# Attention and expert kernel on one core: the last 64 keys scored with 66 stationary columns, the maxima turned in the scores' shape

## Chip, cores and metric

One core of a Trainium2 chip runs the whole program. The metric is device microseconds of one execution; the profile is of one execution. Engines: PE is TensorE (PEld its loading of stationary operands), DVE is VectorE, ACT is ScalarE, POOL is GpSimd, and SP issues DMAs. Each engine takes its instructions in the order of the program.

## The reference

```python
# attention: batch 8, 8 heads, 576 positions, head size 64, float32
scores = (q @ k.T) / sqrt(64)
scores = where(block_i >= block_j, scores, -1e9)     # blocks of 64 positions
attn = exp(scores - scores.max(-1)); attn /= attn.sum(-1) + 1e-9
x = (attn @ v) -> (4608, 512)
# soft mixture: 8 experts, 4 slots each, width 1024
logits = x @ phi
d = softmax over the 4608 tokens; c = softmax over the 32 slots
slot_in = d.T @ x
slot_out[e] = relu(slot_in[e] @ w1[e]) @ w2[e]
x = c @ slot_out
# product block
a = x @ moe2_w1; b = x @ moe2_w2                     # 512 -> 1024 each
out = ((a * b) @ w3) @ w_out                         # 1024 -> 1024 -> 512
```

## The kernel before

The 64 heads of attention are taken as 32 pairs. Queries and keys lie transposed, one head of a pair on partitions 0 to 63 and the other on 64 to 127, so two matmuls of 64 rows run at once, one for each head. Scores stand with keys on the partitions and queries along the row. FP32 products are made from rounded parts: a high part (cast, L483, on ACT) and a low part (difference, L490, on POOL), and each product is three matmuls.

For each pair, `op_M` (L495) multiplies the high parts with queries on the partitions, four groups in four bank pairs, and `op_R` (L504, DVE) takes the maxima of 64 keys each. `op_l2` makes of them the running maximum that a query needs, ten columns. These must become rows: `op_mT` (L516) transposes them into one PSUM bank, `op_mc` (ACT) copies, and `op_mx` (L524) issues three small DMAs that put them into rows 0 and 64 of X. Rows 1 to 5 of X, and the tiles `CT`, are constants of the causal mask.

`op_Q` (L533) makes the scores in four units. In each unit a key tile has three matmuls a head and a fourth, `CT` times X, which subtracts the maximum and adds the mask. Unit 0 holds key tile 1 (queries 128 on, 448 columns) and the last keys, 512 to 575, which only 64 queries see. These last are scored with 128 stationary columns, keys 448 to 575, of which the first 64 are masked. `op_E` (ACT) takes the exponential of a unit, `op_P` (POOL) sums, `op_V` multiplies with the values, `op_SU` makes the row sums, and `op_sb` (DVE) gathers them. Every four pairs are a batch of the tokens; its logits, transposes and slot inputs run under the next pairs.

PSUM has eight banks. A unit or a maxima group takes a pair of them, other products one. The order of everything is made by a planner (`Plan`, L88): each operation has an engine, a duration, its predecessors, banks, and a due time from the tables `OFF`, `EARLY`, `LATE`, `TAIL` and `POST`. It simulates the engines and emits the program in the order found; a matmul's mode (rows for 64-row matmuls, cols, quarters, full) adds a cost where it changes.

The product block's weights don't depend on tokens. `background` (L949) unpacks 64-bit floats into 32-bit ones under the pairs: a load, four DVE operations, and an ACT square, 26 times, for w_out, the first two pieces of w3T, w1 and w2. The other 14 pieces of w3T follow the pairs (`op_rl`, `op_nq`, `op_n`), together with 16 windows of expert weights of 2 MB (`op_wl`). From w3T and w_out, `op_W` makes W = w3 w_out in 192 matmuls that fill TensorE where the plan has time. After the last expert the slots' a and b are multiplied for all slot pairs: `slot_product` (L1188) makes two products and their sum on DVE, and halves the columns of equal slots; `run` (L1212) multiplies this with W to H and then makes the output from products of the combine weights and H.

Where pairs 0 and 1 wait, `run` of the attention (L921) puts matmuls of zeros that keep TensorE busy.

Of the kernel before, what the change touches and what calls it, by code (L numbers as in the profile page):

```python
# [17 lines left out]
S = 576  # L18
# [9 lines left out]
SP = 640  # L28
# [3 lines left out]
def warm(nc, keep, ps, n, w=128):  # L32

    for _ in range(n):
# [3 lines left out]
OFF = dict(ld=(-3671.042, -1992.2911, -303.0511, -1589.0792), ldv=(-930.8255, -774.9205, -2694.8577, 3004.9495),  # L38
           cast=(2024.9564, 3492.1229, 4706.3225, 4642.3979), sub=(829.8094, 2265.7417, 2641.5476, 2007.6771),
           M0=(-206.0862, -217.4342, -265.7846, -210.5146), M1=(-171.9627, -155.0874, -208.7453, -200.1106),  # L40
           M2=(-127.28, -214.9706, -278.1956, -151.8956), M3=(-169.0631, -252.9726, -229.3314, -145.805),
           l2=(-2693.6488, -1083.0339, 305.268, -503.7642), mT=(-95.3927, -48.5566, -124.2345, -87.7389),
           Q0=(84.7224, 29.4226, 39.4315, 30.1907), Q1=(89.7578, 54.2034, 79.5471, 35.3739),
           Q2=(98.4373, 58.5153, 51.2166, 82.5414), Q3=(89.8008, 88.7918, 49.8111, 57.1466),
           P0=(-913.8297, 548.2446, -1367.0333, -777.5844), P3=(-741.4936, 304.0305, -2114.9437, -1607.1186),
           V1=(203.1097, 209.8759, 219.5606, 192.1869), V0=(210.9204, 105.6152, 105.8713, 102.9399),
           SU=(199.7409, 191.2759, 151.163, 120.8971), r=960.7404, sx0=2515.4131, sx1=596.7543, sx2=-224.853, sx3=1870.0829,
           lg=396.7265, lgT=458.8917, cm=1933.1093, cT=701.6961, LTm=-87.1704, dn=451.3287, xn0=454.2761, xn1=453.8451,
           xn2=454.1203, xn3=462.6411, xn4=453.5743, S=599.0796, b=972.45)
EARLY = dict(M=(-1939.2203, -1039.3961, -688.4126, -538.7845), m=(-1036.791, -811.8334, -353.2116, -479.9624),  # L50
           Q=(-544.7669, -532.4325, 0.6058, 2.9171))
LATE = dict(M0=(-16.3677, 49.8754, 121.1889, 106.9067), M1=(34.8112, -16.0442, 130.5073, 45.366),
           M2=(-51.968, -1.3651, 69.8318, 86.3003), M3=(15.7624, 30.6289, -20.4844, 74.7255),
           mT=(51.0406, -15.9257, 149.4984, 95.4908), Q0=(24.9312, 0.9292, 84.621, 21.3772),
           Q1=(34.3074, 5.1476, 72.0112, 23.5192), Q2=(43.4204, 156.7641, 97.6101, 59.7645),
           Q3=(96.7668, 43.761, 104.3689, 4.6122), V0=(73.0635, 78.2534, 59.9265, 67.87),
           V1=(88.439, 24.2563, -33.0555, -8.2603), SU=(47.2236, 52.2312, 59.474, 69.5294),
           P0=(-210.3803, 47.2262, -17.1057, -266.9367), P3=(-25.429, 138.4384, 270.5177, 147.8325), r=-70.1372,
           sx0=-899.6328, sx1=-289.9241, sx2=-157.185, sx3=-1390.0855, lg=58.1323, lgT=222.5747, cm=-2205.5693, cT=18.7186,
           LTm=262.8129, dn=136.0191, xn0=149.6667, xn1=149.7181, xn2=163.6786, xn3=152.9745, xn4=149.6899, S=78.0479)  # L60
TAIL = dict(ts0=55.039, ts1=202.9811, lp0=-73.3871, lp1=57.9615, lp2=92.4441, lp3=101.5796, lt0=13.4395, lt1=90.8232,
           lt2=147.4599, lt3=205.3071, lr0=-343.9437, lr1=23.7771, lr2=98.6037, lr3=141.9388, xp0=129.3181, xp1=247.1579,
           xp2=302.5411, xp3=232.2751, xv0=-298.7287, xv1=321.9726, xv2=413.8655, xv3=-86.0816, chain=305.4669, comb=862.7258)
POST = dict(zm=586.802, W=21.766, We=-46.7975, Wh=312.1576, L=320.647, end=1110.3234, gh=490.5089, wl1=514.8806,
           wl2=114.7633, wl3=350.3128, wl4=-14.0545, wl5=228.0647, wl6=283.632, wl7=180.7612, wl8=598.3248, wl9=-30.7145,
           wl10=-32.1815, wl11=340.3284, wl12=670.2797, wl13=574.1696, wl14=167.9497, wl15=458.1722, rl2=564.6351,
           rl3=415.347, rl4=385.1454, rl5=342.5668, rl6=343.7061, rl7=173.1379, rl8=480.8373, rl9=642.1142, rl10=833.6257,
           rl11=60.6455, rl12=855.0533, rl13=394.0873, rl14=443.1501, rl15=-201.4425, nn2=424.0058, nn3=518.5431,
           nn4=101.2576, nn5=394.7296, nn6=544.1525, nn7=325.031, nn8=-17.0662, nn9=96.1954, nn10=400.0281, nn11=-274.2212,
           nn12=406.7534, nn13=52.5124, nn14=262.381, nn15=-17.5859, ph0=84.5591, ph1=-202.3024, ph2=396.9223, ph3=-565.2237,  # L70
           ph4=395.4213, ph5=351.3727, ph6=617.1742, ph7=572.4085, ph8=653.9999, ph9=374.4742, ph10=862.6272, ph11=286.4333,
           ph12=89.271, ph13=-293.3737, ph14=181.7482, ph15=153.9457, wh0=219.6349, wh1=-487.9067, wh2=444.6471,
           wh3=688.3682, wh4=498.6715, wh5=634.0177, wh6=59.5096, wh7=133.4419)
LOOK = dict(PE=0.0, DVE=1203.38805, ACT=958.21088, POOL=239.37081, SP=467.41166)
WAIT = dict(PE=0.0, DVE=8162.43521, ACT=4947.91525, POOL=3536.23117, SP=12465.53057)
PERIOD, HELD, SLIP, WIN0, WIN1 = 100.0, 30, 0.1, 20, 29
BG0, BGS = 3.0, 1.0
TURN = {"rows": dict(cols=.14, full=.165, quarters=.1), "cols": dict(rows=.205, full=.1, quarters=.06),
        "quarters": dict(rows=.22, full=.03, cols=.06), "full": dict(rows=.147, cols=.05, quarters=.03)}
# [3 lines left out]
MX = ((.262, 1.14), (.199, 1.007), (.14, .73), (.23, .73))  # L83
QK = ((1.25, .92), (1.026, .92), (.583, .6), (.475, .495))
VD = (0.65, 2.06)


class Plan:  # L88
# [3 lines left out]
    def __init__(self, nb):  # L92
# [4 lines left out]
        for n in range(N):  # L97
# [6 lines left out]
            if n == 0:  # L104
                op("kl", "SP", 2.9, lat=2.3, due="ld", late=-7e4)
                op("kc", "ACT", 2.1, at("cast", "kl"), due="cast", late=.1)
# [14 lines left out]
            e, f = ("DVE", .5) if n == N - 1 else ("POOL", 1.)  # L121
# [41 lines left out]
        for j in range(26):  # L163
# [12 lines left out]
    def last(self, N):  # L176
# [4 lines left out]
        for i in range(2):  # L181
            op("ts", i, "PE", .33, [("sb", N - 2 + i)], 1, due=f"ts{i}")
            op("tr", i, "DVE", .5, [("ts", i)] + [("tr", 0)] * i, free="ts", due=f"ts{i}", late=.1)
# [193 lines left out]
class Attn:  # L377
# [62 lines left out]
    def constants(self):  # L440
# [10 lines left out]
        for t in self.xTb:  # L451
            nc.gpsimd.memset(t[64:128, :, S:SP], 0.0)
# [1000 lines left out]
```

## Time and profile before

| | us |
|---|---|
| three runs | 569.20, 571.18, 571.79 |
| median | 571.18 |
| profiled execution | 569.49 |
| its span, first to last instruction | 567.6 |

| engine | busy us | share of the span | instructions |
|---|---|---|---|
| PE | 550.2 | 97% | 5444 |
| PEld | 414.3 | 73% | 5444 |
| DVE | 393.6 | 69% | 716 |
| ACT | 320.9 | 57% | 624 |
| POOL | 334.1 | 59% | 242 |

The busy time of an engine is a mean over stages with different limits, so it is read by stretches: pairs up to about 318 us, expert weights and W up to 427, slot products and H up to 453, the output behind. Matmuls are pipelined and their ends are modelled; the distance between two starts says what one costs. A matmul of FP32 operands that isn't a transpose stands as two instructions. In a timeline row the first number is the start, the second the time from the first start to the last end, and a bracket gives idle time before it and what ended that.

### The profile page before, as it was taken

To read this page: it belongs to the slowest core of one execution; us is meant where nothing else is said; L and a number is where in the kernel's file an instruction comes from. 1 tells how busy PE (TensorE), PEld (TensorE's weight loads), DVE (VectorE), ACT (ScalarE), POOL (GpSimd) and SP (SyncE) were. 2 spreads that over 40 slices of the span, in tenths; PEclk is the share of its full clock that TensorE was granted. 3 is DMA by queue.
4 is the path that set the end of the run, shared out by engine and by line. 5 is a ranking of instruction groups with operands and counts; after the bars stand their busy time and mean duration, and the time that the engine had idled before them with its cause. 6 is when DMAs were issued, how large, how long until landed. Compare 5 with 4: busy or idle time off the path is not lost.

```text
span 567.6 us, 13929 instructions
## 1 busy us (share of the span) xinstructions
PE 550.2 (97%) x5444; PEld 414.3 (73%) x5444; DVE 393.6 (69%) x716; ACT 320.9 (57%) x624; POOL 334.1 (59%) x242
## 2 busy tenths in 40 slices
PE   5999999999999999999999998998999999999997
PEld 3887878787878787878777763563667668888885
DVE  6678877888888988978870888105749776646550
ACT  4656758577686686785866653223532355544451
POOL 5887997987979979979977543103441013323230
PEclk9899999999999999999999998998999999999999
DMA  8355866566558466466354989999722037558622
GB/s 253 92 169 161 238 255 197 160 200 191 176 170 233 138 209 188 160 199 199 117 163 166 384 308 380 429 426 421 286 64 76 1 116 261 192 189 263 200 101 112
DMA packets 39289, 116.96 MB, mean 206 GB/s; under 512 B 5420, under 2 KB 15644, under 8 KB 37160
## 3 DMA queue, kind: packets, MB, share of 16 engines
q1 hardware_dynamic: 39224, 116.07, 59.4%
q8 instruction: 43, 0.70, 0.5%
q14 instruction: 22, 0.18, 0.1%
HBM read 105.75 MB, written 10.45 MB: 205 GB/s over the span
## 4 chain that ended last, share of the span: by engine, by line
PE 85%; DMA 6%; DVE 4%; ACT 2%; POOL 1%; issue 1%; DVEq 0%; POOLq 0%; ACTq 0%; SPq 0%
PE ps L542 20%; PE ps L1287 16%; PE ps L575 15%; PE ps L1066 6%; PE ps L502 5%; PE ps L591 4%; DMA s<-in_w3T 4%; PE ps L1224 3%; PE ps L697 3%; PE ps L1108 2%; DMA raw<-in_qk 2%; PE ps L640 2%; PE ps L1289 1%; PE ps L746 1%; PE ps L1087 1%; PE ps L518 1%
## 5 line engine op out<-in xcount | busy, mean ns | idle before, releaser
L506 DVE TENSOR_REDUCE tc<-ps 128x10 f32<-128x640 f32 (+2 forms) x128 | 122.5, 987 | 33.4 <-PE ps L502 25.8
L550 ACT ACTIVATE s<-ps 128x1024 f32<-128x1024 f32 (+2 forms) x128 | 102.9, 838 | 44.7 <-PE ps L542 34.5
L542 PE MATMUL ps<-set 64*128 64x320 f32 (+4 forms) x1152 | 112.8, 305 | 0.0
L542 PEld LDWEIGHTS ps<-set 64*128 64x128 f32 x1152 | 90.6, 187 | 5.0 <-issue 1.7
L490 POOL TENSOR_TENSOR set<-raw,set 128x1152 fp32r<-128x1152 f32 x32 | 84.9, 2657 | 7.8 <-ACT set L483 5.8
L560 POOL TENSOR_TENSOR tc<-tc,s 128x384 f32<-128x384 f32 (+1 forms) x63 | 80.7, 1281 | 7.0 <-ACT s L550 3.6
L560 POOL TENSOR_TENSOR tc<-s,s 128x640 f32<-128x640 f32 x32 | 49.9, 1560 | 30.4 <-ACT s L550 24.0
L575 PE MATMUL ps<-s,xw 128*64 128x320 f32 (+3 forms) x528 | 63.7, 383 | 0.0
L542 PE MATMUL ps<-shift 64*128 64x320 f32 (+4 forms) x384 | 58.5, 301 | 0.0
L1287 PE MATMUL ps<-H,pB 128*128 128x512 f32 x216 | 53.7, 395 | 0.4 <-POOL pB L1267 0.4
L1267 POOL TENSOR_TENSOR pB<-wx,pB 128x384 fp32r<-128x384 f32 x12 | 16.1, 1342 | 64.4 <-ACT pB L1262 64.4
L1287 PE MATMUL ps<-H,pA 128*128 128x512 f32 x216 | 53.2, 395 | 0.2 <-DVE H L1331 0.2
L502 PE MATMUL ps<-set 64*128 64x320 f32 (+4 forms) x384 | 48.3, 325 | 3.2 <-ACT set L483 3.0
L575 PEld LDWEIGHTS ps<-s,xw 128*64 128x64 f32 x528 | 34.6, 137 | 22.6 <-issue 0.7
L1294 ACT COPY s<-ps 128x512 f32<-128x512 f32 x36 | 21.1, 586 | 51.0 <-PE ps L1289 50.9
L1287 PEld LDWEIGHTS ps<-H,pB 128*128 128x128 f32 x216 | 40.6, 189 | 10.7 <-POOL pB L1267 1.1
L1287 PEld LDWEIGHTS ps<-H,pA 128*128 128x128 f32 x216 | 40.6, 188 | 10.3 <-DVE H L1331 0.5
L483 ACT CAST set<-raw 128x1152 fp32r<-128x1152 f32 x31 | 35.7, 1153 | 4.0 <-DMA raw<-in_qk 4.0
L502 PEld LDWEIGHTS ps<-set 64*128 64x128 f32 x384 | 31.5, 193 | 8.4 <-ACT set L483 3.5
L542 PEld LDWEIGHTS ps<-shift 64*128 64x128 f32 x384 | 36.8, 187 | 0.5
L1040 DVE TENSOR_SCALAR ps<-s 128x512 int32<-128x512 int32 x14 | 9.7, 692 | 34.1 <-DMA s<-in_w3T 33.9
L981 POOL TENSOR_TENSOR s<-vt,s 128x512 fp32r<-128x512 f32 x14 | 17.9, 1281 | 23.6 <-ACT s L983 23.6
(264 smaller groups left out, 1036.7 us busy)
## 6 DMA issues: line engine op xcount, KB each, us to landing
win<-in_moe_w SPq DMA_DIRECT2D x13, 2048.0 KB
raw<-in_qk SPq DMA_DIRECT2D x32, 576.0 KB
vt<-in_moe_w SPq DMA_DIRECT2D x16, 512.0 KB
out<-s SPq DMA_DIRECT2D x16, 512.0 KB
shift<-rr SPq DMA_DIRECT2D x56, 144.0 KB
s<-in_w3T SPq DMA_DIRECT2D x14, 512.0 KB
xw<-in_v SPq DMA_DIRECT2D x22, 320.0 KB
xw<-in_moe_w SPq DMA_DIRECT2D x3, 2048.0 KB
```

The costliest lines, as they stand in the source:

```text
L483: self.nc.scalar.copy(hi, self.raw[n])
L490: self.nc.gpsimd.tensor_tensor(lo, self.raw.pop(n), hi.bitcast(F32), op=ALU.subtract)
L502: self.nc.tensor.matmul(ps[:, h, o:o + kn], lhsT=qh[r, q0:q0 + 128], rhs=kh[r, k0:k0 + kn], start=True, stop=True)
L506: self.nc.vector.tensor_reduce(self.bmb[n % 2][:, :, o:o + m // 64], self.st.pop(("M", n, i))[:, :, 0:m].rearrange("p h (n k) -> p h n k", ...
L542: self.nc.tensor.matmul(ps[:, h, o0:o0 + w], lhsT=lt[r, k] if i < 3 else lt[r], rhs=rt[r, q0:q0 + w], start=i == 0, stop=i == 3)
L550: self.nc.scalar.activation(out=out, in_=ps[:, :, 0:sum(g[3] for g in self.UNITS[u])], func=AF.Exp, scale=SCALE)
L560: eng.tensor_tensor(acc[:, :, lo:hi], a, b, op=ALU.add)
L575: mm(ps[64 * h:64 * h + 64, q0 - lo:q1 - lo], lhsT=v[:, 128 * j + 64 * h:128 * j + 64 * h + 64], rhs=pt[:, h, o:o + q1 - q0], start=j == 0 ...
L591: mm = lambda g, o, rhs, **k: self.nc.tensor.matmul(ps[32 * g:32 * g + 32, o:o + rhs.shape[-1]], lhsT=one, rhs=rhs, **k)
L1066: self.nc.tensor.matmul(self.st["W", f], lhsT=a[:, o], rhs=b, start=j == 0, stop=j == 23)
L1287: nc.tensor.matmul(ps, lhsT=a[:, k, r], rhs=b[:, k], start=k + i == 0, stop=False)
L1294: nc.scalar.copy(o[:, h], bank(u, t))
```

## The change

Unit 0 of the scores starts with one mask product of 512 columns for key tile 1 and the last keys together. X and the constants grow to 640 columns for that: the last 64 queries' columns stand twice. The last keys follow with 66 stationary columns (keys 510 to 575; the two extra rows are masked), then the 448 columns of tile 1. The value rows of the last keys move to partitions 2 to 65. From pair 8 on, the first maxima group also uses 66 columns.

The maxima are turned, for pairs 2 to 31, by two transposes of 64 rows and 66 columns into a pair of banks, and moved by four DMAs. For pairs 0 and 1, ten FP32 matmuls with one stationary column each put each maximum row onto one partition, and ACT (`mc`) and DVE (`mk`) copy from there to X without a DMA.

Two more pieces of w3T go into the background (28 in place of 26). The halving in `slot_product` goes; the first H chunk is scaled by a column `own` instead (`op_ow`). In `run` the copy of X moves behind slice 7's cast. All tables of due times and some planner costs have new values.

```diff
             for i, (d, e) in enumerate(QK):
                 wait = at("Q0") if i else old(n - 2, "V1", "V0", "SU", "P0", "P1", "P3")
-                op(f"Q{i}", "PE", d, at("sub", "mx") + wait, 2, mode="rows")
+                op(f"Q{i}", "PE", d, at("sub") + moved + wait, 2, mode="rows")
...
-            op("mT", "PE", .109, at("l2") + (old(n - 2, "mx") or [("kl", 0)]), 1)
-            op("mc", "ACT", .148, at("mT"), free="mT", due="mT")
-            op("mx", "SP", .625 * 3, at("mc") + old(n - 2, *quarter("Q")) + ([("kc", 0)] if n == 0 else []), lat=2., due="mT", load=.3)
+            if n < 2:
+                op("mT", "PE", 1.3, at("l2") + [("kl", 0)], 2, mode="quarters")
+                op("mc", "ACT", 1.2, at("mT") + [("kc", 0)], due="mT")
+                op("mk", "DVE", 1.2, at("mT") + [("kc", 0)], free="mT", due="mT")
+            else:
+                op("mT", "PE", .12, at("l2") + (old(n - 2, "mx") if n > 3 else []), 2, mode="rows")
+                op("mc", "ACT", .17, at("mT"), free="mT", due="mT")
+                op("mx", "SP", .6 * 4, at("mc") + old(n - 2, *quarter("Q")), lat=2., due="mT", load=.3)
+            moved = at("mx") if n > 1 else at("mc", "mk")
...
-        for j in range(26):
+        for j in range(28):
...
-                op("zm", i, "POOL", .5, win[i])
+                op("zm", i, "POOL", .5, win[i] + [("pl", 3)] * (i == 0))
...
-            if i > 1:
+            if i > 3:
                 op("rl", i, "SP", .43, free[i] if i < 8 else [("W", 24 * (f - 4) + 12 * g + 11)], lat=2.5, load=1.25, due=f"rl{i}")
...
+            m = 66 if c == 0 and n > 7 else 128
             for h in range(2):
                 r = slice(64 * h, 64 * h + 64)
-                self.nc.tensor.matmul(ps[:, h, o:o + kn], lhsT=qh[r, q0:q0 + 128], rhs=kh[r, k0:k0 + kn], start=True, stop=True)
+                self.nc.tensor.matmul(ps[0:m, h, o:o + kn], lhsT=qh[r, q0:q0 + m], rhs=kh[r, k0:k0 + kn], start=True, stop=True)
...
-        self.nc.tensor.transpose(ps, self.m.pop(n).rearrange("p h w -> p (h w)"), self.ident)
+        if n < 2:
+            for w in (0, 1, 2, 3, 4):
+                for h in range(2):
+                    o = 128 * (w % 4)
+                    self.nc.tensor.matmul(ps[32 * h:32 * h + 1, w // 4, o:o + 128], lhsT=m[:, 5 * h + w:5 * h + w + 1], rhs=self.ident, start=True, stop=True)
+        else:
+            for h in range(2):
+                r = slice(64 * h, 64 * h + 64)
+                self.nc.tensor.transpose(ps[0:66, h, 0:64], m[r], self.ident[r, r])
+
+    def rows(self, eng, n, h):
+        ps, X = self.mt[n], self.Xb[n % 2][64 * h:64 * h + 1]
+        p = slice(32 * h, 32 * h + 1)
+        eng(X[:, 64:S], ps[p, 0, 0:512])
+        eng(X[:, S:SP], ps[p, 0, 448:512])
+        eng(X[:, 0:64], ps[p, 1, 0:64])
...
+        self.nc.sync.dma_start(out=X[0:65:64, S:SP], in_=t[3:9:5, 64:128])
         self.nc.sync.dma_start(out=X[0:65:64, 0:64], in_=t[4:10:5, 0:64])
...
+        if u == 0:
+            for h, r in two:
+                mm(h, 0, 512, self.CT[r, 1], X[r, 128:SP], start=True, stop=False)
+            for lt, rt in terms:
+                for h, r in two:
+                    mm(h, 448, 64, lt[r, 510:S], rt[r, 512:S], 66, start=False, stop=False)
+            for i, (lt, rt) in enumerate(terms):
+                for h, r in two:
+                    mm(h, 0, 448, lt[r, 128:256], rt[r, 128:S], start=False, stop=i == 2)
+            return
...
+    def op_ow(self, i, _):
+        self.own = self.attn.small[:, 60:61]
+        self.nc.vector.tensor_reduce(self.own, self.keep["ident"][:, 0:128:4], axis=AX.X, op=ALU.add)
+        self.nc.vector.tensor_scalar(self.own, self.own, -0.5, 1.0, op0=ALU.mult, op1=ALU.add)
...
             nc.vector.tensor_tensor(G, G, T, op=ALU.add)
-            own = cols(G)[:, 0, :, 0]
-            return nc.vector.tensor_scalar(own, own, 0.5, None, op0=ALU.mult).ins
...
                 for i in range(8):
                     h_last(i)
+            if f == 7:
                 nc.scalar.copy(X, Hp[4])
...
-            nc.scalar.copy(Hhi[:, k], Hp[k])
-            nc.vector.tensor_tensor(Hlo[:, k], Hp[k], Hhi[:, k].bitcast(F32), op=ALU.subtract)
+            if k == 0:
+                nc.scalar.mul(Hhi[:, 0], Hp[0], self.own)
+                nc.vector.scalar_tensor_tensor(Hlo[:, 0], Hp[0], self.own, Hhi[:, 0].bitcast(F32), op0=ALU.mult, op1=ALU.subtract)
+            else:
+                nc.scalar.copy(Hhi[:, k], Hp[k])
+                nc.vector.tensor_tensor(Hlo[:, k], Hp[k], Hhi[:, k].bitcast(F32), op=ALU.subtract)
```

## Rows read from the trace of the kernel before

**Rows 1.** Stretch; busy us of PE, PEld, DVE, ACT, POOL; clock; DMA share, GB/s

```profile
0.00:26.00 26.00, 19.90 (x164) 14.64 (x166) 17.19 (x37) 13.38 (x17) 17.10 (x20) 0.87 0.61 188
...
180.30:218.80 38.50, 38.50 (x528) 31.02 (x526) 33.58 (x62) 27.98 (x54) 33.26 (x23) 1.00 0.61 187
...
360.00:400.00 40.00, 37.70 (x254) 20.98 (x251) 9.98 (x15) 8.93 (x21) 5.09 (x4) 0.91 1.00 421
```

**Rows 2.** Waits, 26 to 296 us: us in total, times, longest

```profile
ACT s L550 <- PE ps L542: 32.2, 55, 1.6
```

**Rows 3.** TensorE's timeline, one unit 0: start, us, engine, line, operation

```profile
209.41 0.77 PE L542 MATMUL ps<-set 64*128 64x448 f32 x6
...
210.22 0.41 PE L542 MATMUL ps<-set 64*128 64x64 f32 x6
210.47 0.28 PE L542 MATMUL ps<-shift 64*128 64x64 f32 x2
210.58 0.54 PE L502 MATMUL ps<-set 64*128 64x320 f32 x6
```

**Rows 4.** TensorE's timeline, the end of one pair's value products

```profile
63.00 0.28 PE L579 MATMUL ps<-s,xw 128*64 128x64 f32 x4
63.11 0.82 PE L575 MATMUL ps<-s,vb 128*64 128x256 f32 x8
```

**Rows 5.** TensorE's timeline, one turn of maxima between other transposes

```profile
200.38 0.27 PE L518 MATMUL ps<-ident,wx 128*10 128x128 f32 x1
200.50 0.27 PE L697 MATMUL ps<-ident,wx 128*64 128x128 f32 x1
```

**Rows 6.** Timeline of the first 22 us

```profile
10.21 0.28 PE L518 MATMUL ps<-ident,wx 128*10 128x128 f32 x1
...
14.48 0.64 PE L502 MATMUL ps<-set 64*128 64x320 f32 x2 [2.98 <-ACT set L483]
...
17.04 1.32 PE L542 MATMUL ps<-set 64*128 64x448 f32 x6
```

**Rows 7.** Chain that ended last: start, us, engine and line, instructions

```profile
79.26 1.46 PE ps L640 x64
...
427.17 16.85 PE ps L1224 x72
...
467.38 2.79 PE ps L1287 x12
```

**Rows 8.** Timeline of all engines, 411 to 470 us: a copy of 512 columns

```profile
445.94 0.59 ACT L1321 COPY tc<-ps 128x512 f32<-128x512 f32 x1 [2.61 <-PE ps L1228]
```

**Rows 9.** DVE's timeline, 300 to 400 us

```profile
388.64 0.69 DVE L1040 TENSOR_SCALAR ps<-s 128x512 int32<-128x512 int32 x1 [32.16 <-DMA s<-in_w3T]
```

**Rows 10.** TensorE's timeline, 318 to 430 us

```profile
346.34 1.17 PE L1066 MATMUL ps<-raw,s 128*128 128x512 f32 x4 [2.15 <-DVE vt L1046]
```

**Rows 11.** Timeline of all engines again, slot products and what follows

```profile
423.37 1.58 POOL L981 TENSOR_TENSOR s<-wO,s 128x512 fp32r<-128x512 f32 x1 [7.10 <-ACT s L983]
...
423.84 1.17 DVE L1199 TENSOR_SCALAR g_stage<-g_stage 128x32 f32<-128x32 f32 x1
...
428.15 1.78 DVE L1195 TENSOR_TENSOR g_stage<-tc 128x512 f32<-128x512 f32 x1
...
433.81 0.68 DVE L1197 TENSOR_TENSOR g_stage<-g_stage 128x512 f32<-128x512 f32 x1
434.52 0.20 DVE L1199 TENSOR_SCALAR g_stage<-g_stage 128x32 f32<-128x32 f32 x1
434.62 0.68 DVE L1194 TENSOR_TENSOR g_stage<-tc 128x512 f32<-128x512 f32 x1
...
446.42 0.62 ACT L1206 CAST g_stage<-g_stage 128x512 fp32r<-128x512 f32 x1
...
447.10 1.22 PE L1224 MATMUL ps<-s,g_stage 128*128 128x512 f32 x3 [0.34 <-ACT g_stage L1206]
```

**Rows 12.** The page's costliest groups: exponentials of the scores

```profile
L550 ACT ACTIVATE s<-ps 128x1024 f32<-128x1024 f32 (+2 forms) x128 | 102.9, 838 | 44.7 <-PE ps L542 34.5
```

More of the change, by code (lines that the diff above doesn't have):

```diff
@@ L61 @@
[L61 to L73, printed above, removed]
@@ L76 @@
+LOOK = dict(PE=0.0, DVE=1443.82951, ACT=879.71342, POOL=478.25372, SP=447.13586)
+WAIT = dict(PE=0.0, DVE=10616.85007, ACT=6722.41331, POOL=7334.5673, SP=12439.66901)
 PERIOD, HELD, SLIP, WIN0, WIN1 = 100.0, 30, 0.1, 20, 29
 BG0, BGS = 3.0, 1.0
-TURN = {"rows": dict(cols=.14, full=.165, quarters=.1), "cols": dict(rows=.205, full=.1, quarters=.06),
-        "quarters": dict(rows=.22, full=.03, cols=.06), "full": dict(rows=.147, cols=.05, quarters=.03)}
+TURN = {"rows": dict(cols=.14, full=.165, quarters=.1), "cols": dict(rows=.14, full=.1, quarters=.06),
+        "quarters": dict(rows=.15, full=.12, cols=.06), "full": dict(rows=.147, cols=.05, quarters=.03)}
@@ L105, in __init__ @@
                 op("kl", "SP", 2.9, lat=2.3, due="ld", late=-7e4)
-                op("kc", "ACT", 2.1, at("cast", "kl"), due="cast", late=.1)
+                op("kc", "ACT", 1.9, at("cast", "kl"), due="cast", late=.1)
             op("sub", "POOL", 2.6, at("cast"))
@@ L120, in __init__ @@
             op("P1", "POOL", .96, at("P0"), due="P0", late=.1)
-            e, f = ("DVE", .5) if n == N - 1 else ("POOL", 1.)
+            e, f = ("DVE", .8) if n == N - 1 else ("POOL", 1.)
             op("P3", e, 1.51 * f, at("P0", "E2"))
@@ L182, in last @@
             op("ts", i, "PE", .33, [("sb", N - 2 + i)], 1, due=f"ts{i}")
-            op("tr", i, "DVE", .5, [("ts", i)] + [("tr", 0)] * i, free="ts", due=f"ts{i}", late=.1)
+            op("tr", i, "DVE", .35, [("ts", i)] + [("tr", 0)] * i, free="ts", due=f"ts{i}", late=.1)
         for p in range(NP_B):
@@ L189, in last @@
             op("lr", p, "DVE", .48, [("lt", p), ("tr", p // 3)] + [("la", p - 1)] * (p > 0), free="lt", due=f"lr{p}")
-            op("la", p, "DVE", .27 if p == 0 else .5, [("lr", p)] + [("la", p - 1)] * (p > 0), due=f"lr{p}", late=.1)
+            op("la", p, "DVE", .4 if p == 0 else .7, [("lr", p)] + [("la", p - 1)] * (p > 0), due=f"lr{p}", late=.1)
             op("xp", p, "PE", .545, [("lp", p)], 2, due=f"xp{p}")
@@ L203, in last @@
         op("wT", 0, "PE", .1, [("mS", 0), ("wM", 0)], due="chain", late=.45)
-        op("wb", 0, "DVE", 1.3, [("wT", 0), ("we", 0)], free="wM", due="chain", late=.55)
+        op("wb", 0, "DVE", 1.58, [("wT", 0), ("we", 0)], free="wM", due="chain", late=.55)
         op("ws", 0, "PE", .15, [("wb", 0)], 1, due="chain", late=.7)
-        op("wr", 0, "DVE", .3, [("ws", 0)], free="ws", due="chain", late=.75)
+        op("wr", 0, "DVE", .44, [("ws", 0)], free="ws", due="chain", late=.75)
         op("mI", 0, "PE", 1.13, [("mC", 0)] + [("xv", p) for p in range(NP_B)], 1, mode="quarters", due="chain", late=.6)
@@ L282, in experts @@
         op("aT", 0, "PE", .4, [("ac", 0)], 1, due="end", late=.3)
-        op("aa", 0, "ACT", 1., [("aT", 0)], due="end", late=.4)
-        op("ad", 0, "DVE", 1., [("aT", 0)], due="end", late=.5)
+        op("aa", 0, "ACT", .85, [("aT", 0)], due="end", late=.4)
+        op("ad", 0, "DVE", .85, [("aT", 0)], due="end", late=.5)
         op("af", 0, "SP", 0.01, [("aa", 0), ("ad", 0)], lat=0., free="aT", due="end", late=.6)
         op("g0", 0, "POOL", .4, [("L2", 7)], due="end")
+        op("ow", 0, "DVE", .3, [("L2", 6)], due="end")
         for f in range(4):
```

162 lines of the change are left out of this document (94 added, 68 removed).

## Prediction

> **What bounds the kernel now.** I read the busy time by stage first [rows 1], then the waits [rows 2], then TensorE's timeline. While the 32 head pairs run, TensorE is busy for all of the 38.50 us of a batch of four pairs (one of the eight is shown), at the full clock (granted share 1.00); DVE has 33.58, POOL 33.26, ACT 27.98. ACT's largest wait in that stretch is for TensorE's scores (32.2 us in 55 waits) [rows 2], so the engines behind TensorE stand waiting for it. In this stage a microsecond of TensorE's program order is a microsecond of the span. Three others are bounded otherwise. Before 17 us TensorE waits for data, and the clock's mean is 0.87 [rows 1]. From 360 to 400 us the DMA share is 1.00 at 421 GB/s. From 446 to 467 us a chain through ACT, DVE and POOL is last (the end term below).
>
> **How a score unit is paid.** Two matmuls, one for each head, run at once on 64 rows each; I call that a step. [Rows 3] show unit 0 of one pair. The four steps of 448 columns go from 209.41 to 210.22: 0.81, or 0.20 each. The steps of 64 columns come next, and the last takes from 210.47 to 210.58: 0.11. Streaming 64 columns should take 64/448 of 0.20, 0.03; the 0.11 is the loading of the next step's 128 stationary columns, which such a short step can't hide. The four short steps show 0.36 because the first one's load lay under the mask's 448 columns; the fourth's successor pays its load in the next unit. So 0.81 + 4 × 0.11 = 1.25. With 64 stationary columns, [rows 4] have four matmuls, two steps, from 63.00 to 63.11: 0.055 each.
>
> **(a) Unit 0, all 32 pairs.** After: one mask step of 512 columns (512/448 of 0.20 = 0.23); two steps that wait for 66 columns (taken as those of 64, 0.055 each); one that waits for the 128 columns of the first 448 (0.11); three of 448 (0.61). Sum 1.06, so 0.19 less a pair: 32 × 0.19 = **6.1 us**. The 66-column load itself is in no row. If it costs like 128, the sum is 0.23 + 0.33 + 0.61 = 1.17, 0.08 less (2.6 us in all); if it hides wholly, 0.23 + 0.06 + 0.11 + 0.61 = 1.01, 0.24 less (7.7). I take the row of 64, since 66 is nearest to it. All of this lies on TensorE's order, the path. The 66 columns in the maxima products (pairs 8 on) I cost at nothing: that load already lies under a step of 256 columns and the next load stays at 128; without that cover it would be 0.055 × 24 = 1.3.
>
> *A rule that speaks against (a).* In the rows, halving the columns halves the step. The Trainium skill (TensorE: Matmul & The Clock Gate, Weight-path perf modes) says that fast weight load is on with 128 weights of a type other than FP32. If it were on here, 66 columns would lose it, and (a) would give no more than its lower bound, 2.6; the trace shows no sign of it, 0.11 against 0.055.
>
> **(b) Turning the maxima, pairs 2 to 31.** Now one transpose on the whole array; between others of that shape it costs 0.12 (200.38 to 200.50) [rows 5]. After, two transposes of 64 rows run at once, in the scores' shape; their 66 columns hide under the step before, and the next step's 128 are exposed: 0.06 to 0.11. That gives 0 to 0.05 for each of 30, and the turn may go between scores without changing the array's shape. I take **0.8 us**, between 1.5 gained and 1.5 lost (0.05 the other way, should it stand between steps of another shape). SP issues a fourth small transfer of the rows for each such pair; SP issues nothing else that is late here. The mask now wants the rows 0.6 us earlier in the unit, first and not last. In the due times of the diff the turn stands more than half a pair ahead of its scores.
>
> **(c) Pairs 0 and 1.** Today the turn of pair 0 stands at 10.21, its rows go by DMA, and the first scores begin at 17.04, behind pair 2's maxima products (14.48, which waited for the cast) [rows 6]. After, five steps of two FP32 matmuls of 128 columns: [rows 7] give 1.46 for 64 instructions, four at once, 768 columns in each of four column strips, so 640 columns take 1.2, or 2.4 at the lower clock. Then ACT and DVE copy three pieces each at once; one of 512 columns takes ACT 0.59 [rows 8], so 0.6 to 1.8 for three, 1.1 taken. Scores begin near 13.1 (12.0 to 14.4): 3.9 earlier. Pair 2's products, 2.6 at the low clock (1.3 at full), now stand behind instead of ahead, and the second turn is 1.2 of TensorE's order: 3.9 − 1.3 − 1.2 = **1.4 us**. Bounds: 3.2 gained where the second turn falls in idle time; 1.7 lost where turns run at the low clock and DVE's three copies, with pair 1's maxima queued behind them, hold pair 1's scores up.
>
> **(d) Two more pieces of w3T in the background (28, not 26).** Eight DVE operations of 0.69 [rows 9] and two ACT squares move under the scores: DVE has 4.9 us idle in each batch [rows 1], which hides them; without that cover 5.5. They leave the stretch from 310 to 346 us, where DVE also carries the last batch's chain and where TensorE stood 2.15 for such a piece (346.34) [rows 10]. Their 1.05 MB are 2.5 us at 421 GB/s, counted only if the queue is full at that time. What is late next is the last expert weights: DVE later waits 32.16 for a w3T piece behind them in the queue [rows 9], and those bytes stay. So I take **2.0 us**: bounds 4.7 (2.15 + 2.5) and 1.0 lost (the zeros in the first expert window wait for POOL's split of piece 3).
>
> **(e) The halving in the slot products.** Eight DVE operations go; one took 0.20, and from the sum before it to the next product was 0.71 + 0.10 (433.81, 434.52, 434.62) [rows 11]. A sum followed at once by the next product should take about 0.6, the interval without a dependence: 0.2 × 7 = 1.4 of DVE. TensorE hides that up to 444 us: 72 matmuls in 16.85, 0.234 each, against 0.232 in the product loop [rows 7]. It counts behind that, where ACT's cast for slice 7 (446.42) stands behind the copy of X (0.59 at 445.94), and TensorE waits 0.34 for it (447.10) [rows 8, 11]; the copy is now issued after the cast. The chain behind starts up to 1.4 + 0.59 + 0.34 = 2.3 earlier. I take **1.5 us**, bounds 2.3 and 0; the scale in the first H copy and difference changes no operation count.
>
> *A rule weighed.* The first halving took 1.17, ending with POOL's split (423.37 + 1.58) [rows 11]. The Trainium skill (SBUF — State Buffer, Who interferes with whom) says that DVE and POOL share a port pair and that the later one waits for the whole of the other's instruction, also for an operation with two SBUF inputs. The trace agrees: a product at 428.15 took 1.78. Then 0.97 doesn't go with the halving but passes to the product behind it; counting it as gained would make the sum 1.0 larger. I don't count it.
>
> **The sum.** 6.1 + 0.8 + 1.4 + 2.0 + 1.5 = 11.8. The profiled execution is 569.49 (span 567.6 and 1.9 around it), so 557.7; the median of the three runs is 571.18, 0.3% above it, so on that scale **559.4**. All bounds together would be 19.4 gained to 1.6 lost, less likely than any one.
>
> **Rivals.**
> - *66 columns load no faster than 128* (the rule above is one way): (a) is 2.6, time 562.9. Against it: [rows 4]. Chance 0.10.
> - *Another engine is the bound at once.* POOL is at 33.26 of 38.50, DVE at 33.58 and more with (d). For it: POOL's sums lie between exponentials and the row sums in one order. Against it: the waits [rows 2], and 4.9 us idle against 0.9 saved a batch. Then (a) and (b) give nothing: 566.3. Chance 0.12.
> - *Slower: the turn's pair of banks.* The turn takes two of eight PSUM banks in place of one. If all four pairs are held when it comes up, TensorE's order stands until an exponential empties one: 0.838 on average [rows 12]. At 0.6 for each of 30 turns that is 18 us, 577; it decides from 11.8/30 = 0.39 a turn. Against it: ACT waits for TensorE [rows 2], so pairs come free early. Chance 0.08.
> - *The new order gives the gain back.* All due times change, so every operation may move. 0.35 us of waiting a pair eats 11 us: 568.5 to 571. For it: TensorE shows no idle time to win by order alone, only to lose. Chance 0.10.
>
> **How the numbers follow.** My forecast has 0.60, with its own range of 553 to 565. A measurement of this kernel can tell about 0.5% from no change, 568.3 to 574.0. Faster: 0.60 + 0.10 + 0.12 = 0.82. Same 0.10. Slower 0.08. The range of 8 in 10 takes in the forecast's bounds and the rivals to 566.3 and leaves out the last two: 551 to 567.5.
>
> **What would show it.** (a) right: from the mask's start to the next unit 1.0 to 1.1, short steps 0.055, and a batch of about 37.6 in place of 38.5. Wrong: short steps of 0.11. (b): the line of the turn with two entries a pair among scores, and TensorE never idle before it; the banks' rival shows as TensorE waiting for ACT there. (c): first scores near 13. (d): no idle time for DVE's pieces near 340, the last expert window landing earlier after the end of the pairs. (e): no wait at slice 7, and the product loop starting earlier after slice 0. A batch still at 38.5 with TensorE idle would make the prediction wrong at its main term.

## The result and the profile after

The kernel after takes 564.64 us (median of four, 563.02 to 565.62) against 571.48 for the kernel before (569.20 to 571.95): a ratio of 0.9889, interval 0.9854 to 0.9923. That is 6.8 us by the medians and 4.4 to 8.3 by the interval, where 11.8 were forecast. The profiled execution took 564.84, its span is 562.9 (before 567.6). One of the 12 executions of run 3 below took 1328 us and is not in its ratio.

Marks on TensorE's timeline, each the start of the first instruction named, tell where the time went:

| mark | before | after | difference |
|---|---|---|---|
| first scores | 17.04 | 17.55 | +0.5 |
| row sums of pair 0 | 27.06 | 26.11 | −1.0 |
| row sums of pair 24 | 253.15 | 248.68 | −4.5 |
| last matmuls of scores | 311.50 | 305.18 | −6.3 |
| first expert | 337.39 | 340.83 | +3.4 |
| first product of H | 427.17 | 423.27 | −3.9 |
| steady product loop | 467.38 | 462.11 | −5.3 |
| end of the span | 567.6 | 562.9 | −4.7 |

The pairs gain, the stretch from the last scores to the first expert gives 9.8 back, and from there to H 7.3 return. The 0.6 lost in the loop is no part of the change: twelve of its matmuls take 3.04 here and 3.02 before, but also 3.04 in run 1, whose loop is that of before, and 3.02 in runs 6 and 12, whose loop is that of after.

Stretches of after, columns as in [rows 1]:

```profile
0.00:26.00 26.00, 22.10 (x204) 15.13 (x204) 19.24 (x44) 15.54 (x24) 18.25 (x23) 1.00 0.57 187
172.51:210.75 38.24, 38.10 (x530) 29.96 (x526) 33.53 (x62) 28.19 (x56) 32.99 (x22) 1.00 0.60 188
...
360.00:400.00 40.00, 34.89 (x244) 19.11 (x243) 11.19 (x18) 10.94 (x25) 8.82 (x7) 0.96 1.02 427
```

The batch shown is from one row sum to that of four pairs later. It is 38.24, and TensorE, busy for all 38.50 before, now stands for 0.14 of it. Over five batches the mean is 38.04, against 38.59 before: 0.55 less, where 0.9 were forecast. From 360 to 400 us TensorE is busy for 34.89 in place of 37.70: the loads of the experts still fill the queue (share 1.02), and TensorE has less to do while it waits for them. From the row sums of pair 4 to those of pair 24, by distances between starts, the scores take 1.99 less than before, the turns 2.36 less, and everything else 1.6 more, of which 0.5 is in the maxima products: 2.75 in 20 pairs, 0.14 a pair, where 0.22 were forecast.

TensorE's timeline of after, a turn and one unit 0 (they answer to [rows 3] and [rows 5]):

```profile
204.95 0.25 PE L538 MATMUL ps<-ident,wx 64*66 64x64 f32 x2
205.00 0.60 PE L571 MATMUL ps<-set 64*128 64x256 f32 x6
...
205.93 0.40 PE L571 MATMUL ps<-shift 64*128 64x512 f32 x2
206.17 0.99 PE L571 MATMUL ps<-set 64*66 64x64 f32 x12
206.99 0.37 PE L513 MATMUL ps<-set 64*128 64x448 f32 x2
```

From the mask's start to the next unit 1.06, the number forecast; the turn takes 0.05. (The group of twelve merges the six short matmuls with the six of 448 columns.)

The start of after, TensorE's and DVE's timelines:

```profile
11.23 2.30 PE L534 MATMUL ps<-ident,wx 128*1 128x128 f32 x20
15.08 0.67 PE L513 MATMUL ps<-set 64*128 64x320 f32 x6 [1.55 <-ACT set L493]
15.68 1.26 PE L534 MATMUL ps<-ident,wx 128*1 128x128 f32 x20
...
17.55 0.49 PE L571 MATMUL ps<-shift 64*128 64x512 f32 x2
```

```profile
10.79 0.25 DVE L525 TENSOR_REDUCE wx<-tc 128x10 f32<-128x90 f32 x1
10.95 2.94 DVE L517 TENSOR_REDUCE tc<-ps 128x16 f32<-128x1024 f32 x3
13.92 0.69 DVE L543 CAST shift<-ps 1x512 fp32r<-1x512 f32 x1
```

Both turns and pair 2's products (15.08) stand ahead of the first scores, and DVE's copies stand behind 2.94 us of pair 1's maxima. The clock of 1.00 that the view gives for the first 26 us needs care. The trace of after has no entry of the granted clock before 13.6 us (that of before none before 6.2), and the view counts such time as full. The steps say otherwise. Three matmuls of zeros, before and after:

```profile
7.42 0.49 PE L35 MATMUL ps<-zeros 128*128 128x256 bf16 x3 [0.66 <-DVE tc L506]
```

```profile
7.49 0.80 PE L35 MATMUL ps<-zeros 128*128 128x256 bf16 x3 [0.26 <-DVE tc L517]
```

The last two stand 0.213 apart in after, 0.109 in before. So after ran at the lower level from about 7.5 to 13.6 us, ahead of its first scores; in before the entries have that level from 13.0 to 19.8 us, across them.

The 192 products W of the output weights (`op_W`, L1115 after, L1066 before) by stage: from 300 us to the first expert, to the start of the last expert's last matmul, to the first product of H. Columns: stretch, its length, busy us and number on PE, the same on PEld, clock, DMA share, GB/s. First before, then after:

```profile
300.00:337.39 37.39, 7.03 (x24) 4.05 (x24) 1.00 0.80 310
337.39:410.43 73.04, 35.41 (x124) 23.12 (x124) 0.93 0.93 381
410.43:427.17 16.74, 11.20 (x44) 7.96 (x44) 1.00 0.21 65
```

```profile
300.00:340.83 40.83, 12.14 (x42) 7.20 (x42) 1.00 0.70 260
340.83:408.82 67.99, 32.38 (x117) 20.25 (x116) 0.97 0.93 388
408.82:423.27 14.45, 8.91 (x34) 6.08 (x34) 1.00 0.20 61
```

After does 18 more of them ahead of the first expert and 10 fewer at the end, where nothing covers them: the last stretch is 2.29 shorter, and so is their busy time in it (11.20 and 8.91). This view explains most of what follows.

### The profile page after: what moved, and what is told of

It is laid out like the page before. It is cut to its first block, busy times and chain, and to the rows that moved or that the text cites. A ratio compares the mean times of both kernels' runs of the same rounds, so it can differ in the third digit from the quotient of the medians.

```text
span 562.9 us, 14019 instructions
## 1 busy us (share of the span) xinstructions
PE 545.0 (97%) x5444; PEld 404.0 (72%) x5444; DVE 393.8 (70%) x716; ACT 321.7 (57%) x628; POOL 331.4 (59%) x244
## 5 line engine op out<-in xcount | busy, mean ns | idle before, releaser
L571 PE MATMUL ps<-set 64*128 64x320 f32 (+4 forms) x1152 | 103.9, 298 | 1.4 <-ACT s L594 1.4
L571 PEld LDWEIGHTS ps<-set 64*128 64x128 f32 (+1 forms) x1152 | 82.6, 177 | 7.2 <-ACT s L594 1.9
L571 PE MATMUL ps<-shift 64*128 64x320 f32 (+3 forms) x320 | 51.6, 319 | 0.1
L1319 POOL TENSOR_TENSOR pB<-wx,pB 128x384 fp32r<-128x384 f32 x12 | 14.4, 1204 | 62.7 <-ACT pB L1314 62.7
L513 PE MATMUL ps<-set 64*128 64x320 f32 (+5 forms) x384 | 47.1, 324 | 2.0 <-ACT set L493 1.6
L1089 DVE TENSOR_SCALAR ps<-s 128x512 int32<-128x512 int32 x12 | 8.3, 690 | 45.3 <-DMA s<-in_w3T 45.2
L513 PEld LDWEIGHTS ps<-set 64*128 64x128 f32 (+1 forms) x384 | 31.8, 187 | 8.3 <-ACT set L493 2.3
L571 PEld LDWEIGHTS ps<-shift 64*128 64x128 f32 x320 | 30.8, 187 | 0.8 <-DVE tc L517 0.2
L1319 POOL TENSOR_TENSOR pA<-xw,pA 128x384 fp32r<-128x384 f32 x10 | 12.3, 1230 | 31.6 <-ACT pA L1314 31.6
```

The source lines that it names most:

```text
L513: self.nc.tensor.matmul(ps[0:m, h, o:o + kn], lhsT=qh[r, q0:q0 + m], rhs=kh[r, k0:k0 + kn], start=True, stop=True)
L571: mm = lambda h, o, n, lt, rt, m=128, **k: self.nc.tensor.matmul(ps[0:m, h, o:o + n], lhsT=lt, rhs=rt, **k)
L1319: eng.tensor_tensor(Pl[:, k], raw(u)[1][:, k], Ph[:, k].bitcast(F32), op=ALU.subtract)
```

## Experiments

Each run was timed beside the kernel before; us gained are its ratio times the median of before there (569.7 to 570.8). By the same measure after gains 6.3, give or take 2. The edits are shown in short; places and dependences that go with them are left out.

**1. Unit 0 alone.** In the kernel before, with its tables untouched; X gets its last 64 columns by a fourth transfer, for every pair:

```diff
+ for h, r in two: mm(h, 0, 512, CT[r, 1], X[r, 128:SP], start=True)
+ for lt, rt in terms: mm(h, 448, 64, lt[r, 510:S], rt[r, 512:S], 66)
+ for lt, rt in terms: mm(h, 0, 448, lt[r, 128:256], rt[r, 128:S])
```

> The kernel before, in its own order, with the new unit 0 alone (the mask first over 512 columns, the last 64 keys with 66 stationary columns, the mask row of 640 columns with its fourth small transfer for every pair). The forecast's term (a) says 0.19 us a pair, 32 x 0.19 = 6.1, so about 565.4 in all and a batch of 4 pairs of 37.8 in place of 38.5. First rival: seen from one unit's start to the next it is only 1.174 to 1.063, 0.11 a pair, so 3.6 in all, about 567.9, and a batch of 38.1. Second rival: what the pairs gain is taken back behind them by the loads of the experts, whatever the order there: the pairs end 4 to 6 us earlier and the time stays at 570 to 571.5.

Measured: 0.9965 (0.9942 to 0.9988), 2.0 us. The time is near the first rival's, but not for its reason: the pairs did not become shorter. From pair 4's row sums to pair 24's: 193.14 us, before 192.93. The program of TensorE did become shorter: by distances between starts, scores took 0.96 less in these 20 pairs and the maxima products behind unit 0 took 2.05 less, 3.0 together, 0.15 a pair. The value products took 3.2 more. ACT's and TensorE's timelines show why (ACT's line here, the same of before, TensorE's lines here):

```profile
148.29 0.66 ACT L987 ACTIVATE vt<-vt 128x512 bf16<-128x512 f32 x1 [1.89 <-DMA vt<-in_moe_w]
```

```profile
147.69 0.68 ACT L975 ACTIVATE vt<-vt 128x512 bf16<-128x512 f32 x1 [0.26 <-DMA vt<-in_moe_w]
```

```profile
146.97 0.87 PE L587 MATMUL ps<-s,vb 128*64 128x256 f32 x8
149.25 1.03 PE L587 MATMUL ps<-s,xw 128*64 128x320 f32 x6 [1.41 <-ACT s L697]
```

ACT takes its instructions in order. It stood 1.89 us for a background piece issued at 140.92, the small copies behind it came late, and TensorE stood for them; at 225 us the same again. In the kernel before ACT reached that piece when it had all but landed (it waited 0.26). The pairs became faster, the piece did not: issued 0.3 earlier than before (141.22), it was there 0.6 later. Whether the fourth small transfer of each pair slows it was not tested.

**2. The same, with four ACT squares moved.** Only the place of these squares, and of DVE operations that need them, differs:

```diff
+ for j in (6, 10, 14, 18):   # square of piece j goes behind the next four ACT operations
+     seq = move(seq, ("bm", j), 4)
```

> Unit 0 alone in the order before, as in the first run, with four ACT squares of background pieces (6, 10, 14, 18, those at one place of every batch) issued behind the four ACT operations that followed them; nothing else is moved. In the first run TensorE's own program was 0.15 us a pair shorter (4.8 in 32), but it stood 1.7 and 1.3 us at 147.6 and 225.1 for ACT, which waited for such a piece to land. If that wait is what took the gain, both stalls go and the pairs end about 3 us earlier than there: 565.3, and at least 1.5 under the first run. Rival: TensorE finds another wait at the same pace (POOL or DVE bound), the batch stays at 38.6 and the time at 568.3.

Measured: 0.9943 (0.9929 to 0.9957), 3.3 us, 1.3 more than run 1, with intervals that overlap; the span is 2.2 shorter. Both stalls are gone, and pair 4 to pair 24 takes 190.78, 2.36 less than in run 1. So in the stage of the pairs the wait did take the gain of unit 0. Without it unit 0 is worth 3.3 in this order, not 6.1: the 20 pairs are 2.15 shorter than before, 3.4 in 32.

**3. 128 columns in place of 66**, in the kernel after:

```diff
- mm(h, 448, 64, lt[r, 510:S], rt[r, 512:S], 66, start=False, stop=False)
+ mm(h, 448, 64, lt[r, 448:S], rt[r, 512:S], start=False, stop=False)
- vv[:, 2:66, 512:] = ...      ct[5, 1, 2:66] = 0
+ vv[:, 64:, 512:] = ...       ct[5, 1, 64:] = 0
```

> The kernel after, in its own order, with 128 stationary columns for the last keys in place of 66 (keys 448 to 575, the first 64 of them masked). If the load's length is what the short steps pay, three steps go from 0.049 to 0.109 each, 0.18 a pair: 32 x 0.18 = 5.8 us more, about 570.4. If 66 columns load no faster than 128 (a rival of the forecast), the time stays at 564.6.

Measured: 0.9958 (0.9938 to 0.9978), 2.4 us, so 3.9 of after's 6.3 are lost. The same unit 0 on TensorE's timeline:

```profile
208.00 0.39 PE L571 MATMUL ps<-shift 64*128 64x512 f32 x2
208.23 1.11 PE L571 MATMUL ps<-set 64*128 64x64 f32 x12
209.17 0.37 PE L513 MATMUL ps<-set 64*128 64x448 f32 x2
```

1.17 against 1.06. The three short steps together go from 0.147 to 0.250; the scores of 20 pairs take 1.94 more, 0.10 a pair, 3.1 for 32. That is not the 0.18 expected, since the first of the three takes 0.03 with either. The load is shorter with 66 columns: the rival falls.

**4. The turn on the whole array again**, in the kernel after, pairs 2 to 31:

```diff
- for h in range(2): transpose(ps[0:66, h, 0:64], m[r], ident[r, r])
+ transpose(ps[0:10, 0, 0:128], m[:, 0:10], ident)
```

> The kernel after, in its own order, with one transpose on the whole array for the maxima of pairs 2 to 31, as before, in place of two on 64 rows. The forecast's term (b) would be given back: 0.8 us, about 565.4. Rival, from the lines of the turn in the two traces (3.60 us for 20 turns before, 1.23 after): 0.12 a turn, of which up to 0.04 comes back because the mask behind a turn on 64 rows takes longer, so 0.08 to 0.12 for each of 30: 2.4 to 3.5 us, 567 to 568.1.

Measured: 0.9979 (0.9955 to 1.0003), 1.2 us, so 5.1 of after's 6.3 are lost; by the medians it is 3.9, and the span is 3.8 longer. From pair 4 to pair 24 it takes 194.53 in place of 190.18, 0.22 a pair. In that stretch the line of the turn holds 2.85 more, which is 0.14 each, and about 0.9 are two stalls that after doesn't have (at 161.1 and 222.8). The forecast's 0.8 falls. The rival's 2.4 to 3.5 is near; 3.8 to 5.1 lie above it, but the noise of these differences doesn't exclude it.

**5. The slot products alone**, in the kernel before:

```diff
- own = cols(G)[:, 0, :, 0]; tensor_scalar(own, own, 0.5, ...)
- f == 6: scalar.copy(X, Hp[4])
+ f == 7: scalar.copy(X, Hp[4])
+ scalar.mul(Hhi[:, 0], Hp[0], own); scalar_tensor_tensor(Hlo[:, 0], Hp[0], own, ...)
```

> The kernel before, in its own order, with the change of the slot products alone (no halving, its own scale in the first copy and difference, the copy of X behind slice 7). The forecast's term (e) says 1.5 us, about 570.0. Rival, from the marks of the two traces: the first halving of 1.17 us lies ahead of the first products and counts too, and from the last transpose to the first product 2.1 us went, so 2.1 + 1.4 = 3.5 us, about 568.0.

Measured: 0.9975 (0.9957 to 0.9994), 1.4 us. From the last transpose to the first product of H 7.20, as before; from there to the loop 38.69, before 40.21. The forecast's 1.5 holds, its rival falls.

**6. The old start**, in the kernel after: pairs 0 and 1 turned and sent like the others.

```diff
- if n < 2: op("mT", ..., 1.3); op("mc", "ACT", 1.2); op("mk", "DVE", 1.2)
- moved = at("mx") if n > 1 else at("mc", "mk")
+ moved = at("mx")             # turn, copy and transfers for every pair
```

> The kernel after with pairs 0 and 1 turned like the others and their rows sent by transfers (no third form of the turn, no copies by ACT and DVE). The forecast's term (c) says 1.4 us lost, about 566.0. What the trace of after shows speaks against it: its first scores stand at 17.55 us, 0.5 later than before, and only the first row sums are 0.95 earlier, at a full clock in place of 0.86. Rival: no change within 0.5, first scores at 17 us, 564.6, or up to 1 us faster, 563.6, since the second turn of 1.3 us and the copies leave the order.

Measured: 0.9883 (0.9860 to 0.9906): the same as after, the rival. Yet the start is not without effect. Pair 4's row sums come at 60.88, in after at 58.51, although the first scores stand at 17.68 and 17.55. The granted clock is at its lower level here from 7.8 to 21.4 us, in after at the full one from 13.6 us on, and so a step of 448 columns in the first scores takes 0.37 here and 0.20 in after. The 2.4 us are still 2.1 at pair 24 and gone at the last scores (305.31 and 305.20). In after ACT stood for a background piece in between, and TensorE for ACT (ACT's line, TensorE's line, both of after):

```profile
286.47 0.66 ACT L1022 ACTIVATE vt<-vt 128x512 bf16<-128x512 f32 x1 [1.50 <-DMA vt<-in_moe_w]
```

```profile
287.66 0.71 PE L571 MATMUL ps<-set 64*128 64x320 f32 x6 [1.40 <-ACT s L594]
```

With the old start ACT waited 0.18 for the same piece. So most of the lead, 1.4 of 2.1, goes where the piece and not the start sets the time.

**7. 26 pieces**, in the kernel after:

```diff
- for j in range(28):          # background
+ for j in range(26):
- if i > 3: op("rl", i, ...)   # w3T behind the pairs
+ if i > 1: op("rl", i, ...)
```

> The kernel after with the two pieces of w3T taken out of the background again (26 pieces, not 28; pieces 2 and 3 come behind the pairs, through the common staging tile, as before). The forecast's term (d) says 2.0 us lost, about 566.6, between 569.3 and 563.6. From the trace of after the stretch from the first refill of an expert window to the last expert's second product was 66.0 us against 71.1 before, of which 2.5 are the bytes of two pieces: a full return of it would be 5.0, 569.6. Rival: the loads of the experts wait for the first expert anyway and the two pieces fit in the 9.9 us that the queue stood idle from 320 to 345 us: no change, 564.6.

**8. 28 pieces**, part (d) alone, in the kernel before:

```diff
- for j in range(26):          # background
+ for j in range(28):
- if i > 1: op("rl", i, ...)   # w3T behind the pairs
+ if i > 3: op("rl", i, ...)
```

> The kernel before with part (d) alone: 28 pieces in the background in its own order. The forecast's term (d) says 2.0 us gained, about 569.5, between 566.8 and 572.5. Taking the pieces out of the kernel after cost 11.6 us; if that is what two pieces are worth in any order, this run falls to about 560. Rival, from the run of all parts in the old due times: the old times don't fit more work, and the two pieces cost something, 572 to 576, because 8 DVE operations now stand between the steps of the last pairs' chain.

Measured: 1.0088 (1.0057 to 1.0119), 5.0 slower than before, for 26 pieces in the new order; 1.0188 (1.0160 to 1.0216), 10.7 slower, for 28 in the old. Taking two pieces out costs 11.3, putting two in costs 10.7, and no expectation came near either. The profiled execution of run 7 is one of its two fastest (572.79 of 572.75 to 578.55), so its trace shows 7.9 of the 11.3. The products W of the two, stages as above, first run 7 and then run 8:

```profile
300.00:340.95 40.95, 6.59 (x24) 4.12 (x24) 0.97 0.69 261
...
410.00:431.54 21.54, 16.00 (x65) 11.90 (x65) 1.00 0.16 51
```

```profile
300.00:343.66 43.66, 1.66 (x6) 1.05 (x6) 0.88 0.62 242
...
417.44:437.91 20.47, 15.61 (x64) 11.71 (x64) 1.00 0.17 54
```

Each leaves 64 or 65 products for the end, where before has 44 and after 34. In run 8 the first expert also comes 6.3 later than before and the last one 7.0: TensorE was idle up to 3.61 us at a time in the chain to the first, with few products to fill the time. Both runs price two pieces in tables that were made for the other number: in run 7 the two pieces have the due times of before among new ones, in run 8 the tables were made for 26. What two pieces are worth where the tables are made for them was not tested.

**9. All parts with the old due times**, and **10. the old parts with the new due times**:

```diff
  OFF, EARLY, LATE, TAIL, POST, LOOK, WAIT: the other kernel's tables, no other edit
```

> All parts of the change, ordered by the due times of the kernel before (the tables of offsets alone are put back). If the new due times give gain back (the forecast's last rival), the parts now bring more than 6.8: 560 to 563. If the old times are those that don't fit the parts, as in the run of unit 0 alone, where TensorE stood 1.7 and 1.3 us for an ACT that waited for a background piece, the gain is mostly lost: 566 to 572, with waits of TensorE in the stage of the pairs and an expert stage that begins later than 341 us.

> The parts of the kernel before, ordered by the due times of the kernel after (the tables of offsets alone are taken over): the fourth corner beside before, after and the run of all parts in the old due times. If the gain is the new order's and not the parts', this run comes near after: 564 to 566. If parts and due times fit only each other, it is slower than before, as the other mixed corner was by 13 us: 575 to 590, with waits of TensorE in the stage of the pairs.

| | old due times | new due times |
|---|---|---|
| old parts | 1 (570.3 and 570.8 us) | 1.0529 (1.0510 to 1.0549) |
| new parts | 1.0235 (1.0209 to 1.0260) | 0.9889 (0.9854 to 0.9923) |

Measured: 13.4 and 30.2 slower, both beyond what was expected. All parts together don't gain without the tables, nor the tables without the parts. Run 9 looks like run 8: 6 products W ahead of the first expert, which comes at 345.88, and 82 behind the last, busy for 19.70 there. So much of its loss is likely part (d), which alone cost 10.7 in this order, while (a) and (e) alone gained in it (runs 1, 2 and 5); the planner's costs go with the parts here. In run 10 TensorE is idle for 2.75 and 4.33 us at a time among the pairs (up to 134.67 and 221.23), waiting for ACT's casts, and its last scores come at 330.85.

**11 and 12. Two other orders behind the pairs**, in the kernel after; only numbers of `LATE`, `TAIL` and `POST` differ.

```diff
- LATE, TAIL, POST = those of after
+ LATE, TAIL, POST = two other sets
```

> The kernel after with other due times for the last four pairs, the chain behind them and the experts, and no other edit: the value products of the last two pairs and the steps that need them stand before the last batch's own transposes, so that the chain to the first expert starts earlier. If the gain of the pairs is lost in that chain (last scores to first expert 35.4 us, 25.7 before), the first expert begins 2 to 4 us before 340.8 and the time falls by 2 to 4, to 560.6 to 562.6. Rival: what ends last is the loads of the experts and the products of the output weights that are left over, so the time stays at 564.6 although the first expert is earlier.

> As the run before, with a third set of due times that moves the first expert about as far and leaves the order of the last expert's loads closer to that of after. By the first theory 561 to 563, by the rival 564.6.

Measured: run 11 0.9919 (0.9890 to 0.9948), 4.6; run 12 **0.9847** (0.9819 to 0.9875), 8.7: 561.29 us, all its executions (560.38 to 562.11) under all of after's (from 563.02), though the two were timed beside different runs of before and the intervals of their ratios overlap. Products W of run 12, stages as above:

```profile
300.00:337.25 37.25, 9.20 (x31) 5.21 (x31) 1.00 0.71 276
337.25:405.13 67.88, 34.10 (x120) 21.15 (x120) 0.97 0.94 390
405.13:420.35 15.22, 10.36 (x41) 7.39 (x41) 1.00 0.29 92
```

Its first expert stands at 337.25, 3.6 before after's, although its last scores come 4.5 later (309.71), and its first product of H stands at 420.35, 2.9 before. So the tail of after did hold 2 to 3 us. But an early first expert is not enough. Run 11 has it at 338.01 and its H at 423.85, later than after; in its chain 21 products W stand behind the first expert:

```profile
342.13 1.92 PE ps L1137 x16
344.06 5.04 PE ps L1095 x21
349.36 1.91 PE ps L1116 x32
```

The second expert begins there at 349.36, in run 12 at 344.17. So run 12 came out by the first theory of that expectation, run 11 by its rival.

## Why the prediction was right in sign and too large

The 564.64 us lie inside the forecast's own range (553 to 565), at its upper end. That is in part luck: of the five terms one was right, two were too large, one was several times too small, and one has no fixed sign, and the order that joins them was taken as a risk only.

- **What bounds the kernel.** Right for the pairs: less program on TensorE made them shorter. Incomplete in one respect. "The engines behind TensorE stand waiting for it" [rows 2] holds on average, but ACT's order contains waits that TensorE doesn't set, the landings of background pieces. A wait of 0.26 us in before doesn't show that 1.89 follow when the pairs become faster. Runs 1 and 2 show it.
- **(a), 6.1: mechanism right, size off.** Unit 0 takes 1.06 as forecast. The load that the last short step leaves to its successor, argued for in the sum of 1.25, was there: the maxima products behind it fell by 2.05 in 20 pairs. What was mis-sized is what stands ahead of the mask. In half the pairs it comes behind a short step or a turn and takes 0.31 to 0.34, not 0.235. So 0.15 a pair in the program of run 1, 4.8 in all, and 3.3 in time (run 2). After itself keeps less of it: its order places the maxima products elsewhere, and over the same 20 pairs they take 20.89, before 20.37 and in run 1 18.32. Of the two ways to read (a) in after, undoing the columns alone gives 3.9 (run 3), and the scores' 1.99 in 20 pairs give 3.2. The column term is right: in after the two later steps of the three take 0.059 and 0.060 between starts, forecast 0.055; with 128 columns 0.11. The Trainium skill (TensorE: Matmul & The Clock Gate, LDWEIGHTS) counts a load by its columns alone, at 1.2 columns a ns; an estimate by it is 55 ns for 66 and 107 for 128. The trace agrees, with 59 to 60 and 109 to 112. The prediction's rival, by which 66 columns load no faster than 128, falls with run 3: 0.147 against 0.250 for the three short steps.
- **(b), 0.8: wrong row.** It measured 3.5 by its line and 3.8 to 5.1 by undoing it (run 4). [Rows 5] show a turn of 0.12 between other transposes on the whole array. That is the cheapest place: of 20 turns before, five took 0.11 and fifteen 0.20, since most stand between steps of another shape. Another of before, two microseconds later on its timeline:

```profile
202.90 0.27 PE L518 MATMUL ps<-ident,wx 128*10 128x128 f32 x1
203.10 0.87 PE L542 MATMUL ps<-set 64*128 64x448 f32 x6
```

  The mean of 20 is 0.180 before and 0.062 after; (0.180 − 0.062) × 30 = 3.5. (One of after's 20 stands with 0.32, where steps behind it are missing from the trace; the others' mean is 0.05, which gives 3.9.) A mean over all of them was to be had and was not taken; 1.5 was too low as an upper bound. The pair of banks costs next to nothing that the trace shows: of the turns of pairs 2 to 31 one has TensorE idle ahead of it (0.28 us at 25.93), so that rival falls.
- **(c), 1.4: failed at its first step**, "scores begin near 13.1". They begin at 17.55. The turn came at 11.23, not 10.21, behind more of DVE's reductions. It took 2.30, near the upper end of the bound, with steps of 0.213 where those of the second turn take 0.109: it ran at the lower level of the clock. DVE's copies stood behind pair 1's maxima, the reverse of what the lower bound names. And pair 2's products with the second turn stayed ahead of the scores, where the forecast let them follow. What gain there was came with the clock, whose lower stretch lay ahead of the first scores and not across them, and most of it ended in the wait at 286 us (run 6). The 0.87 of [rows 1] is too high as a mean of the start, since the first 6.2 us have no entry and the zeros' steps of 512 columns take 0.427 up to 3.9 us and 0.213 behind it. The bounds, 3.2 gained and 1.7 lost, follow from no sum that is shown.
- **(d), 2.0: not a term.** Its sign depends on the order: put into the old one, two pieces lose 10.7 (run 8); taken out of the new one, they lose 11.3 (run 7). How much of that is tables made for the other number is open. The forecast asked whether DVE has time for eight operations under the scores, and it has (busy for 33.53 of 38.24). The stall of 2.15 for a piece [rows 10] is gone too. It did not ask how many of the 192 W products are left when the experts are done. The two pieces change when products become possible, and each product left at the end is some 0.25 us on the path (11.20 for 44).
- **(e), 1.5: right.** 1.4 alone (run 5). The 0.97 of the first halving passed on, as the prediction said it would: in run 5 and in after the product behind POOL's split takes 1.79. No wait for the cast of slice 7 is left.
- **The rival "the new order gives the gain back"** was half right. The order behind the pairs gives back 9.8 at the first expert, and 2 to 3 of it need not be (run 12). But as a whole the new order is what lets the parts gain together: with the old one they lose 13.4 (run 9). The prediction took the due times as a risk only. It should have taken parts and due times as one change.
- **The sum.** Measured alone, (a) 3.3, (b) 3.5 to 5.1, (c) 0 and (e) 1.4 make 8.2 to 9.8; the total is 6.3 to 6.8. These are runs in two orders, each with a noise of 1 to 2 us, and (d) has no place in the sum. What is missing, 1.4 to 3.5, is about what run 12 wins by order alone. That it is the same time is argued, not shown.

## What to carry to other kernels

When all engines follow one order made by due times, a part need not have a price of its own (here two pieces of background cost 10.7 put into one order, and 11.3 taken out of the other). Find first which filler work (here the W products) is left uncovered at the end, and which waits for loads stand in an engine's order with less than a microsecond to spare. A microsecond saved ahead of such a wait can be lost in it. Where an operation occurs many times, take the mean of its start-to-start distances over all its neighbours; the one clean row can be the cheapest, as here.

## What was not expected of the hardware

- A background piece of 512 KB was there some 7.3 us after its issue (140.92 to about 148.2, run 1), at a DMA share of 0.60 over the pairs, and in before within 6.5 (141.22 to 147.69). Faster pairs did not bring it sooner.
- The load of a long next operand isn't lost when a step is too short to cover it at once: the first step of 448 columns behind the short ones takes 0.284, the others 0.20. By the starts it is paid one step later.
- The turn of pair 0 takes 0.213 a step of two instructions, that of pair 1 0.109, half of it, though the view of stretches gives a granted clock of 1.00 for both. The trace has no entry of the clock before 13.6 us, so the view's 1.00 there says nothing; the steps show the lower level (1.2 GHz) for the first turn and the full one (2.4 GHz) for the second.
